# A list schedule that makes GpSimd and VectorE take turns, loads V and weights behind K, and closes with a fence

## The chip, the cores and the metric

The kernel runs on one NeuronCore of a Trainium2 chip. The metric is the device time of one execution in microseconds (us). The median of three runs before the change is 532.61 us (532.23 to 536.52). The engines are named as the profile names them: PE (TensorE, matrix products), DVE (VectorE), ACT (ScalarE), POOL (GpSimd) and SP (the queue that issues most DMA loads). PE writes to PSUM, of which this kernel uses eight banks, four tagged "a" and four tagged "t".

## The reference

Three layers follow each other on B=2 batches of S=768 rows:

```
scores = q k^T / 8 + bias;  keep = (first n_global columns) or (0 <= row - column < n_local)
a = softmax(where(keep, scores, -1e9));  x = a v                # 8 heads of 64
h = (x^T U V)^T;  u = x + h                                     # U: 768x32, V: 32x768
x = u + relu(u w_ch1) w_ch2                                     # 512 -> 2048 -> 512
k = relu(mix(x, mu_k) w_k)^2;  r = sigmoid(mix(x, mu_r) w_r);  out = r * (k w_v)
```

mix(x, mu) = mu * x + (1 - mu) * (x shifted by one row). n_global is 8 and n_local is 96, so a block of 128 rows needs a narrow band of K columns and the first few.

## The kernel before, in words

**Front.** Attention runs on eight pairs of heads (four pairs p for each of two batches b, numbered pp = 0 to 7), each in six blocks i of 128 rows. For a pair, SP loads Q (384 KB), K (768 KB) and V (768 KB). For each block PE makes the scores (`s`, line 433), DVE adds the bias and takes the extremum (`P`, `nm`, line 441), ACT takes the exponential (line 449), DVE inverts the sums after three blocks (`sm`, lines 454 and 455), POOL scales the rows (`P`, line 460, two steps a block), PE transposes (`tp`, line 467), and ACT or DVE copies the result out of PSUM (`PT`). After three blocks PE multiplies with the even rows of V (`xa`, `xb`, line 482, step `pa`), after six with the odd rows (line 493, step `pb`); then ACT and DVE copy `xa` and `xb` to `yp` (step `y`).

Beside that the front converts weights. They arrive as float64 in `stg` (512 KB a piece); one conversion is `cvt` (DVE, line 616), `c1` (ACT, line 621), `c2` and `c3` (DVE, lines 625 and 629), and a split into a high part (`hi`, ACT, line 633) and a low part (`lo`, POOL, line 636). Nine conversions belong to the front: one piece for U and V, four for `w1s`, four for `w2s`. When batch 0 is done, the front also transposes it (`xtp`, line 734), multiplies with U and V (`gps`, `hps`), adds h to `yp` (`hd`, `he`, line 788), splits the result (`sh` on ACT, `sl` on POOL, line 821), and does the first product with w_ch1 (`aps`, line 852, steps `ch`; `rs`, lines 856 and 860).

**What sets the order.** `Flow` (lines 52 to 138) is a list scheduler that runs while the program is built. `pairs` and `rest` give it 644 steps with a kind, a rank, the steps they need (`after`), the steps that must only be planned first (`behind`) and the buffers (`Tok`) they take or use. `COST` gives for each kind the engine, how long it holds that engine and after how long its result can be used. `run` takes again and again the step that can start first (lower rank first within `SLACK`), and emits its instructions; so each engine's queue in the front is in the planned order, and `tc.manual_schedule` keeps it so. A step that needs a buffer of a full pool waits for a fixed one: the oldest taken, whether it is free or not (line 97). The plan of before lets POOL and DVE steps run beside each other at will.

**Behind the front**, from line 984 on, no plan is made: the framework's own scheduler orders the instructions by their priority and may also put them between those of the front where the engine's queue has, by its reckoning, room. There batch 1 is transposed (`xtp`), and a steady stretch alternates `aps` (48 matmuls) and `bps` (line 874, 48 matmuls) over four groups of weights and three chunks of 512 rows, with the conversions of the next groups woven in (`bg`); then come `kps`, `prs`, `pvs` for the last layer.

Of the kernel before, what the change touches and what calls it, by code (L numbers as in the profile page):

```python
# [7 lines left out]
F32 = mybir.dt.float32  # L8
# [5 lines left out]
ALU = mybir.AluOpType  # L14
# [11 lines left out]
FLOWLOG = None  # L26
BIG = 1.0e9 * 256.0
# [24 lines left out]
class Flow:  # L52

    COST = {
# [4 lines left out]
        "nm": [("POOL", 0.42, 0.50)], "pt": [("ACT", 0.37, 0.52), ("DVE", 0.47, 0.60)],  # L61
        "y": [("ACT", 0.38, 0.54), ("DVE", 0.47, 0.60)], "xt": [("ACT", 0.49, 0.64), ("DVE", 0.60, 0.74)],
        "cvt": [("DVE", 0.40, 0.48)], "c1": [("ACT", 0.59, 0.73)], "c2": [("DVE", 0.61, 0.74)],
# [8 lines left out]
    SWITCH, SLACK, RATE, LAND = 0.13, 0.06, 400.0, 2.0  # L72

    def __init__(self, caps, now, queue):
        self.caps, self.now, self.queue = caps, dict(now), queue
        self.steps, self.order = [], {p: [] for p in caps}
# [5 lines left out]
    def taken(self, pool, n, done=0.0):  # L82
        for _ in range(n):
            t = Tok(pool)
            t.done = done
            self.order[pool].append(t)

    def ready(self, x):

        if any(a.end is None for a in (*x.behind, *x.after)):  # L90
            return None
        old, count = [], {}
# [8 lines left out]
        for eng, hold, lat in self.COST[x.kind]:  # L101
# [3 lines left out]
            out.append((max([go] + [t.done for t in old]), eng, hold, lat))  # L105
        return out

    def run(self, log=None):
        left, self.mode = list(self.steps), None
        while left:  # L110
            cand = {}
            for x in left:
                for go, eng, hold, lat in self.ready(x) or ():
                    cand.setdefault(eng, []).append((go, x, hold, lat, eng))
# [7 lines left out]
            go, x, hold, lat, eng = best  # L122
            go, eng, hold, lat = min(self.ready(x), key=lambda y: y[0] + y[3])
            x.start, x.eng, x.free = go, eng, go + hold
            self.now[eng] = go + hold
            if eng == "PE":
                self.mode = self.MODE.get(x.kind, 0)
            if eng == "SP":
                self.queue = max(self.queue, go + self.LAND) + lat / self.RATE
                x.end = self.queue  # L130
            else:
                x.end = go + lat
            for t in x.new:
                self.order[t.pool].append(t)
# [45 lines left out]
def body(tc, out, q, k, v, lim, UV, w1, w2, mu_kr, wk, wv, wr):  # L180
    nc = tc.nc
    with ExitStack() as ctx:
# [9 lines left out]
        y = yp.rearrange("p k (b s) -> p k b s", b=2)  # L192
# [107 lines left out]
        def attention_windows(pool, actx, cctx, bctx, bank, evict, rest, xt_p):  # L300
# [156 lines left out]
            def s_norm(pp, i, x):  # L457
                z = st[pp]
                Px = z["P"][i][:, 192 * (1 - x):192 * (2 - x)]
                nc.gpsimd.tensor_scalar(out=Px, in0=Px, scalar1=z["sm"][:, i, x:x + 1], scalar2=1.0,  # L460
                                        op0=ALU.mult, op1=ALU.mult)
# [40 lines left out]
            def pairs(fl):  # L502

                out, ls, lm, lt, lp, lx = [], None, None, None, None, None
                for pp in range(NPR):
                    R = 10.0 * pp
                    q, kk, vt = Tok("q"), Tok("k"), Tok("v")
                    nm, sm = Tok("nm"), Tok("sm")
                    lq = lk = None
                    if pp < 2:  # L510
                        for t in (q, kk):
                            fl.order[t.pool].append(t)
                    else:
                        lq = fl.add("dq", lambda pp=pp: load_q(pp), new=[q], rank=R - 12)
                        lk = fl.add("dk", lambda pp=pp: load_k(pp), after=[lq], new=[kk], rank=R - 12)
                    lv = fl.add("dk", lambda pp=pp: load_v(pp), new=[vt], rank=R - 4)
# [15 lines left out]
                    for h in range(2):  # L532
                        m = fl.add("sm", lambda pp=pp, h=h: s_sum(pp, 3 * h, 3 * h + 3),
                                   after=[e[i, x] for i in range(3 * h, 3 * h + 3) for x in range(2)], use=[sm], rank=R + 3 * h / 6)
                        for i in range(3 * h, 3 * h + 3):
                            n[i] = [fl.add("nm", lambda pp=pp, i=i, x=x: s_norm(pp, i, x), after=[m], use=[P[i], sm],
                                           rank=R + 2 + i / 6) for x in range(2)]
                    R += 8
                    for i in range(NT):
                        t = Tok("t")  # L540
                        a = fl.add("tp", lambda pp=pp, i=i: t_mm(pp, i), after=n[i] + [a if i else None], new=[t], use=[P[i]], rank=R + i / 6, behind=[lt, lx if i == 2 else None])
# [14 lines left out]
                return out  # L556
# [8 lines left out]
            with tc.manual_schedule(engines={mybir.EngineType.PE, mybir.EngineType.Activation, mybir.EngineType.DVE,  # L565
                                             mybir.EngineType.Pool, mybir.EngineType.SP}):
                fl = Flow({"a": 4, "t": 4, "P": 10, "PT": 8, "q": 2, "k": 2, "v": 2, "nm": 3, "sm": 3, "stg": 3, "cvt": 2,
                           "cvc": 4, "zt": ZT},
                          {"PE": 5.9, "ACT": 6.6, "DVE": 6.4, "POOL": 10.0, "SP": 3.1}, 7.6)
                fl.taken("P", 7, 6.4)  # L570
                fl.taken("t", 1, 5.9)
                fl.taken("nm", 1)
                fl.taken("sm", 1)
                rest(fl, pairs(fl))
                fl.run(FLOWLOG)

        def path(general):
            if general:
                attention_general()
            with ExitStack() as pctx:  # L580
# [25 lines left out]
                def conv_steps(shape, hi, lo, plain=None):  # L606
# [28 lines left out]
                    def low(z):  # L635
                        nc.gpsimd.tensor_tensor(out=lo, in0=z["c"].bitcast(F32), in1=hi.bitcast(F32), op=ALU.subtract)  # L636
# [174 lines left out]
                def u_split(c, kk, mk, part=None):  # L811
# [4 lines left out]
                    if part == "high" or part == "low":  # L816
# [3 lines left out]
                        else:  # L820
                            nc.gpsimd.tensor_tensor(out=u[:, 1, kk, a:e], in0=ys, in1=u[:, 0, kk, a:e].bitcast(F32),
                                                    op=ALU.subtract)
# [91 lines left out]
                else:  # L914
                    actx, bctx, cctx = ExitStack(), ExitStack(), ExitStack()

                    def rest(fl, ends):
# [3 lines left out]
                        def conversion(r):  # L921
# [3 lines left out]
                            ds = fl.add("ds", lambda: z.update(stage(src)), new=[toks["st"]], rank=r - 12)  # L925
                            d = {}
                            for kind, f in steps:
# [4 lines left out]
                                d[kind] = fl.add(kind, lambda f=f: f(z), after=after, new=[toks[x] for x in new],  # L932
# [3 lines left out]
                        uvd = conversion(24)  # L936
                        w1d = [conversion(r) for r in (34, 44, 54, 64)]
# [9 lines left out]
                        R = 41.0  # L947
# [21 lines left out]
                        for kk in range(4):  # L969
                            h = fl.add("sh", lambda kk=kk: u_split(0, kk, slot_a, "high"), after=[adds[kk, 0]], rank=R + 1)  # L970
                            sp.append([h, fl.add("sl", lambda kk=kk: u_split(0, kk, slot_a, "low"), after=[h], rank=R + 1)])
# [8 lines left out]
                    attention_windows(pool, actx, cctx, bctx, bank, evict, rest, xt_p)  # L980
# [137 lines left out]
```

## Time and profile before

| what | us |
|---|---|
| median of three runs | 532.61 |
| the profiled execution's own time | 532.49 |
| its span, first to last instruction | 530.7 |
| PE busy (95%) | 506.5 |
| DVE busy (58%) | 306.7 |
| ACT busy (41%) | 220.2 |
| POOL busy (35%) | 187.3 |

The span is the time from the first to the last instruction; 1.8 us lie around it. An engine's busy time counts its instructions, not its waits. A row of a timeline gives start, length, engine, line, operation, output and inputs; in brackets stand the idle time of the engine before the row and what ended it. "PEclk" is the TensorE clock that was granted, as a share of the full 2.4 GHz.

### The profile page before, as it was taken

To read this page: it belongs to the slowest core of one execution; us is meant where nothing else is said; L and a number is where in the kernel's file an instruction comes from. 1 tells how busy PE (TensorE), PEld (TensorE's weight loads), DVE (VectorE), ACT (ScalarE), POOL (GpSimd) and SP (SyncE) were. 2 spreads that over 40 slices of the span, in tenths; PEclk is the share of its full clock that TensorE was granted. 3 is DMA by queue.
4 is the path that set the end of the run, shared out by engine and by line. 5 is a ranking of instruction groups with operands and counts; after the bars stand their busy time and mean duration, and the time that the engine had idled before them with its cause. 6 is when DMAs were issued, how large, how long until landed. Compare 5 with 4: busy or idle time off the path is not lost.

```text
span 530.7 us, 8670 instructions
## 1 busy us (share of the span) xinstructions
PE 506.5 (95%) x3314; PEld 413.1 (78%) x3314; DVE 306.7 (58%) x665; ACT 220.2 (41%) x515; POOL 187.3 (35%) x247
## 2 busy tenths in 40 slices
PE   7789988799999999999999999999999999999995
PEld 4568667678888888888888888887888888888884
DVE  7689998749995563825547655798033623252110
ACT  6899985416532404104031321543931442044100
POOL 7577598004440402104031402644731442044100
PEclk9999999799999999999999999999999999999998
DMA  8887534500553040401304130041001000100001
GB/s 327 320 288 264 204 103 158 161 2 0 173 183 122 16 143 0 159 0 38 121 1 159 33 126 0 1 158 41 0 21 40 22 1 21 40 20 1 21 21 46
DMA packets 13586, 47.18 MB, mean 89 GB/s; under 512 B 1760, under 2 KB 2144, under 8 KB 13536
## 3 DMA queue, kind: packets, MB, share of 16 engines
q1 hardware_dynamic: 13248, 46.28, 25.5%
q8 instruction: 28, 0.46, 0.4%
q10 hardware_dynamic: 288, 0.26, 0.2%
q14 instruction: 22, 0.18, 0.1%
HBM read 43.39 MB, written 3.15 MB: 88 GB/s over the span
## 4 chain that ended last, share of the span: by engine, by line
PE 77%; DVE 12%; DMA 5%; ACT 1%; issue 1%; POOL 1%; SPq 0%; DVEq 0%; POOLq 0%; ACTq 0%
PE aps L852 23%; PE bps L874 21%; PE pvs L1057 12%; PE kps L1027 10%; PE prs L1046 6%; DMA KK<-in_k_dram 5%; DVE cvc L625 3%; DVE cvc L629 2%; DVE P L441 1%; PE tp L467 1%; DVE cvt L616 1%; PE s L433 1%; DVE yp L878 1%; DVE xt L686 1%; DVE mix L1014 1%
## 5 line engine op out<-in xcount | busy, mean ns | idle before, releaser
L852 PE MATMUL aps<-us,w1s 128*128 128x512 f32 x576 | 133.3, 390 | 0.0
L874 PE MATMUL bps<-rs,w2s 128*128 128x512 f32 x576 | 132.5, 389 | 0.0
L874 PEld LDWEIGHTS bps<-rs,w2s 128*128 128x128 f32 x576 | 108.1, 188 | 23.2 <-PE gps L752 0.8
L852 PEld LDWEIGHTS aps<-us,w1s 128*128 128x128 f32 x576 | 107.9, 188 | 22.2
L856 ACT ACTIVATE rs<-aps 128x512 fp32r<-128x512 f32 x48 | 28.1, 593 | 92.9 <-PE aps L852 92.9
L1027 PE MATMUL kps<-mix,wk 128*128 128x512 f32 x288 | 66.1, 389 | 0.5 <-ACT kf L1031 0.5
L1027 PEld LDWEIGHTS kps<-mix,wk 128*128 128x128 f32 x288 | 54.0, 188 | 12.1 <-ACT kf L1031 0.9
L1057 PE MATMUL pvs<-wv,kh 128*128 128x512 f32 (+1 forms) x208 | 61.9, 373 | 0.0
L625 DVE SCALAR_TENSOR_TENSOR cvc<-cvc,cvt 128x512 uint32<-128x512 uint32 (+1 forms) x53 | 51.1, 965 | 8.8 <-ACT cvc L621 7.7
L860 DVE SCALAR_TENSOR_TENSOR rs<-aps,rs 128x512 fp32r<-128x512 f32 x48 | 32.6, 684 | 39.4 <-ACT rs L856 39.4
L621 ACT ACTIVATE cvc<-stg 128x512 f32<-128x512 f32 (+1 forms) x53 | 35.1, 671 | 48.4 <-DMA stg<-in_w_dram 22.7
L878 DVE TENSOR_TENSOR yp<-bps,yp 128x512 f32<-128x512 f32 (+1 forms) x64 | 33.9, 550 | 31.2 <-PE bps L874 31.2
L460 POOL TENSOR_SCALAR P<-P,sm 128x192 f32<-128x192 f32 x96 | 45.0, 489 | 19.4 <-ACT P L449 7.7
L1009 POOL TENSOR_SCALAR mixt<-yp,mu 128x512 f32<-128x512 f32 (+1 forms) x32 | 21.5, 678 | 74.2 <-DVE mixf L1011 29.6
L636 POOL TENSOR_TENSOR w1s<-cvc,w1s 128x512 fp32r<-128x512 f32 x16 | 23.8, 1505 | 62.5 <-ACT w1s L633 62.5
L629 DVE SCALAR_TENSOR_TENSOR cvc<-stg,cvc 128x512 uint32<-128x512 uint32 x52 | 45.4, 880 | 0.8
L636 POOL TENSOR_TENSOR w2s<-cvc,w2s 128x512 fp32r<-128x512 f32 x16 | 24.0, 1526 | 60.8 <-ACT w2s L633 57.7
L449 ACT ACTIVATE P<-P,nm 128x192 f32<-128x192 f32 x96 | 42.6, 449 | 3.0 <-DVE nm L441 2.9
L1057 PEld LDWEIGHTS pvs<-wv,kh 128*128 128x128 f32 x208 | 38.1, 188 | 6.9
L1037 POOL TENSOR_TENSOR kl<-kf,kh 128x512 fp32r<-128x512 f32 x24 | 31.0, 1292 | 30.6 <-ACT kh L1036 30.6
L1057 PE MATMUL pvs<-wv,kl 128*128 128x512 f32 (+1 forms) x104 | 38.8, 373 | 0.0
L1011 DVE SCALAR_TENSOR_TENSOR mixf<-yp,mu,mixt 128x512 f32<-128x512 f32 (+1 forms) x32 | 20.3, 653 | 29.8 <-POOL mixt L1009 29.7
(113 smaller groups left out, 594.7 us busy)
## 6 DMA issues: line engine op xcount, KB each, us to landing
stg<-in_w_dram SPq DMA_DIRECT2D x32, 512.0 KB, 4.2
vin<-in_v_dram SPq DMA_DIRECT2D x8, 768.0 KB, 5.8
KK<-in_k_dram SPq DMA_DIRECT2D x7, 768.0 KB, 6.9
stg<-in_wk_dram SPq DMA_DIRECT2D x8, 512.0 KB, 4.2
stg<-in_wv_dram SPq DMA_DIRECT2D x8, 512.0 KB, 3.7
out_dram<-sg SPq DMA_DIRECT2D x11, 256.0 KB, 2.0
QS<-in_q_dram SPq DMA_DIRECT2D x7, 384.0 KB, 5.5
stg<-in_wr_dram SPq DMA_DIRECT2D x4, 512.0 KB, 4.0
```

The costliest lines, as they stand in the source:

```text
L449: nc.scalar.activation(out=Px, in_=Px, func=ACTF.Exp, scale=-1.0, bias=z["nm"][:, i, x:x + 1], accum_out=z["sm"][:, i, x:x + 1])
L460: nc.gpsimd.tensor_scalar(out=Px, in0=Px, scalar1=z["sm"][:, i, x:x + 1], scalar2=1.0, op0=ALU.mult, op1=ALU.mult)
L621: nc.scalar.activation(out=z["c"].bitcast(F32), in_=parts(z)[1].bitcast(F32), func=ACTF.Copy, scale=2.0 ** -112)
L625: nc.vector.scalar_tensor_tensor(out=z["c"], in0=z["c"], scalar=3, in1=z["t"], op0=ALU.logical_shift_left, op1=ALU.bitwise_or)
L629: nc.vector.scalar_tensor_tensor(out=z["c"] if plain is None else plain, in0=parts(z)[1], scalar=0x80000000, in1=z["c"], op0=ALU.bitwise_a ...
L636: nc.gpsimd.tensor_tensor(out=lo, in0=z["c"].bitcast(F32), in1=hi.bitcast(F32), op=ALU.subtract)
L852: nc.tensor.matmul(rs[g, c, f], lhsT=wsl(("w1", g), lw, kk, f * 128, 128), rhs=us[c][:, lx, kk, :], start=(kk == 0 and n == 0), stop=(kk = ...
L860: nc.vector.scalar_tensor_tensor(out=r[:, 1, f, :], in0=rs[g, c, f], scalar=0.0, in1=r[:, 0, f, :].bitcast(F32), op0=ALU.max, op1=ALU.subt ...
L874: nc.tensor.matmul(ps, lhsT=wsl(("w2", g), lw, f, o * 128, 128), rhs=r[:, lx, f, :], start=(n == 0), stop=(n == 11))
L878: nc.vector.tensor_tensor(out=ys, in0=ps[:, a:e], in1=ys, op=ALU.add)
L1027: nc.tensor.matmul(ps, lhsT=wsl("wk", lw, kk, f * 128, 128), rhs=xk[:, lx, kk, :], start=(n == 0), stop=(n == 11))
L1057: nc.tensor.matmul(pv, lhsT=ks[c][lx][:, f, t * 128:(t + 1) * 128], rhs=wsl("wv", lw, f, c0, c1 - c0), start=(n == 0), stop=(n == 23))
```

## The change

The planner is changed, the steps are the same 644. (1) A common time `port` is kept: a POOL step, and a DVE step of the kinds in `PORT`, starts only when the one before it of either engine has ended. Three kinds that were POOL's alone (`nm`, `lo`, `sl`) may go to DVE at a penalty. (2) Q and K of the pairs 2 to 7 are added ahead of everything else; a V load is `behind` the V before it and the K of the next pair, a weight load `behind` a K. (3) A pool gives the buffer whose last user was planned longest ago among those that are free. (4) The first product with V (`pa`) needs no longer all six transposes planned first, nor the third transpose the product; the third and fourth group of `ch` wait for the last scores. (5) A fence: whatever is traced behind the front is issued, on PE, ACT, DVE and POOL, behind the front's last instruction on that engine.

```diff
     COST = {
-        "nm": [("POOL", 0.42, 0.50)],
+        "nm": [("POOL", 0.40, 0.46), ("DVE", 0.25, 0.36, 1.2)],
-        ... "lo": [("POOL", 1.25, 1.35)], ... "sl": [("POOL", 1.15, 1.25)],
+        ... "lo": [("POOL", 1.28, 1.38), ("DVE", 0.62, 0.75, 1.5)], ... "sl": [("POOL", 1.25, 1.35), ("DVE", 0.62, 0.75, 1.5)],
...
-    SWITCH, SLACK, RATE, LAND = 0.13, 0.06, 400.0, 2.0
+    PORT = {("DVE", k) for k in ("cvt", "c2", "c3", "sm", "nm", "lo", "sl", "small")}
+    SWITCH, SLACK, RATE, LAND = 0.13, 0.06, 390.0, 2.1
...
-        for t in x.new:
-            n = len(self.order[t.pool]) + count.get(t.pool, 0) - self.caps[t.pool]
-            count[t.pool] = count.get(t.pool, 0) + 1
-            if n >= 0:
-                old.append(self.order[t.pool][n])
-        if any(u.end is None for t in old for u in t.users):
-            return None
+        for pool in {t.pool for t in x.new}:
+            free = [t for t in self.live[pool] if all(u.end is not None for u in t.users)]
+            free.sort(key=lambda t: max([u.turn for u in t.users], default=-1))
+            n = sum(t.pool == pool for t in x.new) + len(self.live[pool]) - self.caps[pool]
+            if n > len(free):
+                return None
+            old += free[:max(n, 0)]
...
+            if eng == "POOL" or (eng, x.kind) in self.PORT:
+                go = max(go, self.port)
...
+            if eng == "POOL" or (eng, x.kind) in self.PORT:
+                self.port = go + hold
...
+                loads = {}
+                for pp in range(2, NPR):
+                    loads[pp] = [Tok("q"), Tok("k")]
+                    lq = fl.add("dq", lambda pp=pp: load_q(pp), new=loads[pp][:1], rank=10 * pp - 12)
+                    loads[pp].append(fl.add("dk", lambda pp=pp: load_k(pp), after=[lq], new=loads[pp][1:2], rank=10 * pp - 12))
...
-                    lv = fl.add("dk", lambda pp=pp: load_v(pp), new=[vt], rank=R - 4)
+                    lv = fl.add("dk", lambda pp=pp: load_v(pp), new=[vt], rank=R - 4, behind=[lv, loads[pp + 1][2] if 0 < pp < NPR - 1 else None])
...
-                        a = fl.add("tp", ..., behind=[lt, lx if i == 2 else None])
+                        a = fl.add("tp", ..., behind=[lt])
...
-                    last = a
+                    last = None
...
                 fl.run(FLOWLOG)
+                ends = {x.engine: x for x in nc.cur_bb.bb.instructions}
+                return [ends[e] for e in (mybir.EngineType.PE, mybir.EngineType.Activation, mybir.EngineType.DVE,
+                                          mybir.EngineType.Pool)]
...
-                        uvd = conversion(24)
-                        w1d = [conversion(r) for r in (34, 44, 54, 64)]
+                        uvd = conversion(24, lks[0])
+                        w1d = [conversion(r, lk) for r, lk in zip((34, 44, 54, 64), lks[1:])]
...
-                                           new=[t] if kk == 0 else [], use=[t], rank=100 + f)
+                                           new=[t] if kk == 0 else [], use=[t], rank=100 + f,
+                                           behind=[last_s] if f >= FB else [])
...
-                    attention_windows(pool, actx, cctx, bctx, bank, evict, rest, xt_p)
+                    for x in attention_windows(pool, actx, cctx, bctx, bank, evict, rest, xt_p):
+                        fence.enter_context(tc.issue_after(x))
```

Three places of the new order follow; line numbers of the changed kernel are some 10 to 20 higher for the same statement. The first is DVE at the end of the front, where the front's own last steps are the `rs`, `PT`, `hps` and `yp<-xb` rows. Before:

```order
296 L860 SCALAR_TENSOR_TENSOR rs<-aps,rs 128x512
297 L616 TENSOR_SCALAR cvt<-stg 128x512
298 L625 SCALAR_TENSOR_TENSOR cvc<-cvc,cvt 128x512
299 L616 TENSOR_SCALAR cvt<-stg 128x512
300 L629 SCALAR_TENSOR_TENSOR cvc<-stg,cvc 128x512
301 L860 SCALAR_TENSOR_TENSOR rs<-aps,rs 128x512
302 L625 SCALAR_TENSOR_TENSOR cvc<-cvc,cvt 128x512
303 L616 TENSOR_SCALAR cvt<-stg 128x512
304 L629 SCALAR_TENSOR_TENSOR cvc<-stg,cvc 128x512
305 L625 SCALAR_TENSOR_TENSOR cvc<-cvc,cvt 128x512
306 L686 COPY yp<-xb 128x6x64
307 L788 TENSOR_TENSOR yp<-hps,yp 128x256 x4
```

And now:

```order
296 L705 COPY yp<-xb 128x6x64
297 L705 COPY PT<-tp 128x384
298 L634 TENSOR_SCALAR cvt<-stg 128x512
299 L705 COPY PT<-tp 128x384
300 L643 SCALAR_TENSOR_TENSOR cvc<-cvc,cvt 128x512
301 L647 SCALAR_TENSOR_TENSOR cvc<-stg,cvc 128x512
302 L705 COPY yp<-xb 128x6x64
303 L634 TENSOR_SCALAR cvt<-stg 128x512 x2
304 L643 SCALAR_TENSOR_TENSOR cvc<-cvc,cvt 128x512
```

Counted from the start, row 295 of before is the front's ninth and last `c3`; the `cvt`, `c2` and `c3` of rows 297 to 305 except the `rs` belong to the weights behind the front (`w1s` of group 1). Now rows 298, 300 and 301 are the front's ninth conversion, and the foreign ones begin at row 303, behind the last `yp<-xb`. The addition `yp<-hps` for the columns 512 to 767 is done further ahead.

The second place is ACT in the same stretch. Before:

```order
86 L621 ACTIVATE cvc<-stg 128x512
87 L856 ACTIVATE rs<-aps 128x512
88 L621 ACTIVATE cvc<-stg 128x512
89 L684 COPY yp<-xa 128x6x64
90 L621 ACTIVATE cvc<-stg 128x512
91 L684 COPY PT<-tp 128x384 x3
92 L684 COPY yp<-xa 128x6x64
```

And now:

```order
75 L876 ACTIVATE rs<-aps 128x512 x4
76 L703 COPY yp<-xa 128x6x64
77 L703 COPY PT<-tp 128x384
78 L651 CAST w2s<-cvc 128x512
79 L703 COPY PT<-tp 128x384
80 L703 COPY yp<-xa 128x6x64
81 L651 CAST w2s<-cvc 128x512
82 L639 ACTIVATE cvc<-stg 128x512
```

The three `cvc<-stg` of before in rows 86, 88 and 90 are conversions behind the front; now the first of them is row 82, behind the last `yp<-xa`.

The third place is SP from the V load of pair 0 on (`vin` is V, 768 KB a load; `stg<-in_w` 512 KB, `stg<-in_UV` 384 KB). Before:

```order
6 L329 DMA vin<-in_v_dram 128x1536 x2
7 L703 DMA stg<-in_UV_dram 128x384
8 L666 DMA stg<-in_w_dram 128x512
9 L206 DMA mu<-in_mu_dram 128x8
10 L666 DMA stg<-in_w_dram 128x512
11 L318 DMA QS<-in_q_dram 128x768
12 L324 DMA KK<-in_k_dram 128x1536
```

And now:

```order
6 L340 DMA vin<-in_v_dram 128x1536
7 L217 DMA mu<-in_mu_dram 128x8
8 L685 DMA stg<-in_w_dram 128x512 x3
9 L1115 TENSOR_LOAD flag_i
10 L1115 ISA x2
11 L329 DMA QS<-in_q_dram 128x768
12 L335 DMA KK<-in_k_dram 128x1536
13 L340 DMA vin<-in_v_dram 128x1536
```

The second V load moved behind the K of pair 2, the U and V piece further down, and a third `stg<-in_w` ahead. The load of the flag that chooses the program's path, which stood behind the K of pair 3, now stands ahead of the Q of pair 2.

## Rows read from the trace of the kernel before

**Rows 1.** Stretches: busy us (instructions) of PE, PEld, DVE, ACT, POOL; clock; DMA; GB/s.
```profile
0.00:21.20 21.20, 15.01 (x221) 9.42 (x221) 13.47 (x79) 16.47 (x62) 15.46 (x58) 1.00 0.92 350
21.20:62.30 41.10, 38.11 (x764) 29.95 (x766) 36.58 (x159) 38.51 (x141) 27.69 (x57) 1.00 0.70 254
62.30:91.20 28.90, 25.84 (x341) 20.13 (x330) 27.36 (x72) 22.95 (x66) 24.82 (x33) 1.00 0.42 132
91.20:102.30 11.10, 6.49 (x110) 5.63 (x111) 9.58 (x19) 3.35 (x7) 0.44 (x1) 0.69 0.60 184
...
102.30:530.70 428.40, 421.07 (x1898) 348.02 (x1892) 219.70 (x338) 138.91 (x241) 118.91 (x100) 1.00 0.17 55
```

**Rows 2.** PE's waits from 0 to 103 us: us in total, times, longest.
```profile
PE s L433 <- DMA KK<-in_k_dram: 5.2, 5, 2.1
PE tp L467 <- POOL P L460: 4.1, 5, 1.2
PE hps L783 <- ACT yp L684: 3.8, 1, 3.8
```

**Rows 3.** Timeline of PE at the end of the front.
```profile
95.00 0.58 PE L783 MATMUL hps<-uv 96*128 96x256 f32 x1 [3.80 <-ACT yp L684]
96.39 0.58 PE L783 MATMUL hps<-uv 96*128 96x256 f32 x1 [0.81 <-DVE yp L686]
96.81 2.79 PE L467 MATMUL tp<-ident,P 128*128 128x128 f32 x12
```

**Rows 4.** Timeline of ACT, 93 to 96 us.
```profile
93.91 0.67 ACT L621 ACTIVATE cvc<-stg 128x512 f32<-128x512 f32 x1 [2.36 <-DMA stg<-in_w_dram]
94.48 0.47 ACT L684 COPY yp<-xa 128x384 f32<-128x384 f32 x1
```

**Rows 5.** Timeline of DVE, 90 to 96 us.
```profile
90.62 1.57 DVE L625 SCALAR_TENSOR_TENSOR cvc<-cvc,cvt 128x512 uint32<-128x512 uint32 x1
...
93.66 0.67 DVE L625 SCALAR_TENSOR_TENSOR cvc<-cvc,cvt 128x512 uint32<-128x512 uint32 x1
...
95.79 0.54 DVE L686 COPY yp<-xb 128x384 f32<-128x384 f32 x1
```

**Rows 6.** Stretch, as Rows 1, around the fall of the clock.
```profile
93.50:100.40 6.90, 4.59 (x30) 3.86 (x32) 5.51 (x13) 3.00 (x6) 0.00 (x0) 0.51 0.67 183
```

**Rows 7.** Timeline of PE, rows between 14 and 67 us.
```profile
14.83 0.55 PE L467 MATMUL tp<-ident,P 128*128 128x128 f32 x3 [1.18 <-POOL P L460]
...
21.20 1.53 PE L433 MATMUL s<-KK,QS 64*64 64x192 f32 x32 [1.66 <-DMA KK<-in_k_dram]
...
30.51 1.53 PE L467 MATMUL tp<-ident,P 128*128 128x128 f32 x12
...
40.21 0.99 PE L433 MATMUL s<-KK,QS 64*64 64x192 f32 x16 [2.13 <-DMA KK<-in_k_dram]
...
66.61 1.12 PE L467 MATMUL tp<-ident,P 128*128 128x128 f32 x6 [1.11 <-POOL P L460]
```

**Rows 8.** Stretch, as Rows 1, ahead of the scores of pair 2.
```profile
18.00:21.00 3.00, 1.54 (x72) 1.33 (x68) 0.91 (x3) 3.00 (x14) 2.43 (x7) 1.00 1.03 424
```

**Rows 9.** Timeline of POOL: the flag, the low parts of w2s.
```profile
10.02 0.21 POOL L219 TENSOR_SCALAR flag_i<-flag_f 1x1 int32<-1x1 f32 x1
...
84.17 4.86 POOL L636 TENSOR_TENSOR w2s<-cvc,w2s 128x512 fp32r<-128x512 f32 x3
90.31 1.34 POOL L636 TENSOR_TENSOR w2s<-cvc,w2s 128x512 fp32r<-128x512 f32 x1 [1.28 <-ACT w2s L633]
```

**Rows 10.** POOL by line: count, min/median/max ns, first and last start.
```profile
L460 POOL TENSOR_SCALAR P<-P,sm x96: 418/425/1372, 10.5 to 82.8; 128x192 f32<-128x192 f32 x96
L636 POOL TENSOR_TENSOR w1s<-cvc,w1s x4: 1271/1274/1287, 41.7 to 75.0; 128x512 fp32r<-128x512 f32 x4
```

**Rows 11.** Stretches, as Rows 1, just behind the front.
```profile
102.30:107.00 4.70, 4.70 (x42) 3.01 (x36) 3.32 (x8) 3.74 (x9) 0.00 (x0) 1.00 0.37 115
107.00:120.00 13.00, 12.57 (x58) 10.12 (x56) 6.18 (x12) 2.52 (x6) 0.00 (x0) 1.00 0.00 1
```

More of the change, by code (lines that the diff above doesn't have):

```diff
@@ L26 @@
 FLOWLOG = None
+UR = 41.0
+FB = 2
 BIG = 1.0e9 * 256.0
@@ L85, in taken @@
             t.done = done
-            self.order[pool].append(t)
+            self.live[pool].append(t)
     def ready(self, x):
@@ L112, in run @@
             for x in left:
-                for go, eng, hold, lat in self.ready(x) or ():
-                    cand.setdefault(eng, []).append((go, x, hold, lat, eng))
+                for go, eng, _, _, later, _ in self.ready(x) or ():
+                    cand.setdefault(eng, []).append((go + later, x))
             assert cand, [(x.kind, x.rank) for x in left][:9]
@@ L132, in run @@
                 x.end = go + lat
+            for t in old:
+                self.live[t.pool].remove(t)
             for t in x.new:
-                self.order[t.pool].append(t)
+                self.live[t.pool].append(t)
+            x.turn = len(self.steps) - len(left)
             left.remove(x)
@@ L506, in pairs @@
                     R = 10.0 * pp
-                    q, kk, vt = Tok("q"), Tok("k"), Tok("v")
+                    q, kk, vt = *(loads[pp][:2] if pp in loads else (Tok("q"), Tok("k"))), Tok("v")
                     nm, sm = Tok("nm"), Tok("sm")
-                    lq = lk = None
+                    lk = loads[pp][2] if pp in loads else None
                     if pp < 2:
                         for t in (q, kk):
[L512 to L515, printed above, removed]
-                    lv = fl.add("dk", lambda pp=pp: load_v(pp), new=[vt], rank=R - 4)
+                            fl.live[t.pool].append(t)
+                    lv = fl.add("dk", lambda pp=pp: load_v(pp), new=[vt], rank=R - 4, behind=[lv, loads[pp + 1][2] if 0 < pp < NPR - 1 else None])
                     e, P, PT, X, tp, o = {}, {}, {}, [Tok("t"), Tok("t")], {}, []
@@ L540, in pairs @@
                         t = Tok("t")
-                        a = fl.add("tp", lambda pp=pp, i=i: t_mm(pp, i), after=n[i] + [a if i else None], new=[t], use=[P[i]], rank=R + i / 6, behind=[lt, lx if i == 2 else None])
+                        a = fl.add("tp", lambda pp=pp, i=i: t_mm(pp, i), after=n[i] + [a if i else None], new=[t], use=[P[i]], rank=R + i / 6, behind=[lt])
                         lt = a
@@ L555, in pairs @@
                                 for x in range(2)])
-                return out
+                return out, [loads[pp][2] for pp in range(2, NPR)], ls
             wins = masks()
@@ L579, in path @@
                 attention_general()
-            with ExitStack() as pctx:
+            with ExitStack() as pctx, ExitStack() as fence:
                 def pool(name, bufs, side=None, stack=pctx):
@@ L633, in high, with low @@
                         nc.scalar.copy(out=hi, in_=z["c"].bitcast(F32))
-                    def low(z):
-                        nc.gpsimd.tensor_tensor(out=lo, in0=z["c"].bitcast(F32), in1=hi.bitcast(F32), op=ALU.subtract)
+                    def low(z, eng="POOL"):
+                        engine = nc.vector if eng == "DVE" else nc.gpsimd
+                        engine.tensor_tensor(out=lo, in0=z["c"].bitcast(F32), in1=hi.bitcast(F32), op=ALU.subtract)
                     return [("cvt", cvt), ("c1", c1), ("c2", c2), ("c3", c3)] + ([("hi", high), ("lo", low)] if plain is None else [])
@@ L809, in path, with u_split @@
                 us = {}
-                def u_split(c, kk, mk, part=None):
+                def u_split(c, kk, mk, part=None, eng=None):
                     if c not in us:
@@ L915, in path, with rest, conversion @@
                     actx, bctx, cctx = ExitStack(), ExitStack(), ExitStack()
-                    def rest(fl, ends):
+                    def rest(fl, ends, lks, last_s):
                         fl.add("dm", constants, rank=30)
                         fl.add("small", complement, after=[fl.steps[-1]], rank=30)
-                        def conversion(r):
+                        def conversion(r, behind=None):
                             src, steps = bgq.pop(0)
@@ L924, in conversion @@
                             toks = {"st": Tok("stg"), "t": Tok("cvt"), "c": Tok("cvc")}
-                            ds = fl.add("ds", lambda: z.update(stage(src)), new=[toks["st"]], rank=r - 12)
+                            ds = fl.add("ds", lambda: z.update(stage(src)), new=[toks["st"]], rank=r - 12, behind=[behind])
                             d = {}
```

39 lines of the change are left out of this document (22 added, 17 removed), and 2 rows, old and new, of the table COST.

## The prediction

> **What bounds the kernel now.** I read the stretches first [rows 1], to see where PE, the busiest engine, still stands still. From 102.30 to the end it is busy 421.07 of 428.40 us; little is to be had there. The front, 102.30 us long, has PE busy 85.45 us, so 16.85 us idle: 6.19 before 21.20, 2.99 up to 62.30, 3.06 up to 91.20, and 4.61 of only 11.10 us after that. This last stretch also has a granted clock of 0.69. All that a new order of the front can give lies in these idle times and in that clock.
>
> Next the waits of PE there [rows 2]. The scores wait five times for K (5.2 us), the transposes five times for the scaled `P` of POOL (4.1), one `hps` waits 3.80 us for ACT's `yp<-xa`, and the next 0.81 us for DVE's `yp<-xb` [rows 3]. The last two make the whole 4.61.
>
> Then I asked what ACT and DVE did while PE waited. ACT had a `cvc<-stg` directly ahead of `yp<-xa`, and that had stood 2.36 us for a weight's DMA [rows 4]. It is a conversion from behind the front, put by the framework's scheduler into a queue in which a copy was due. DVE likewise had steps of these conversions, 0.67 us each, directly ahead of `yp<-xb` [rows 5]. PE pays twice: from 93.50 to 100.40 the granted clock is 0.51, the 1.2 GHz level, with PE busy 4.59 us [rows 6], and it fell behind the idle time that began at 91.20.
>
> **The change part by part. A, the fence.** It keeps all these conversions behind the front's last instruction on their engine; in the new order the copies of `xa` and `xb` stand ahead of every foreign row on ACT and DVE. Without the wait for the weight's DMA the copies can follow PE. Of the idle 4.61 us I leave 0.6, about one copy (0.54 [rows 5]) that PE has to wait for: 4.0 gained. The clock: twelve transposes took 2.79 us at the low level [rows 3] and 1.53 at the high one [rows 7], so at least 1.26 is lost, and at most half of 4.59, which is 2.3; I take the middle, 1.8. Together **A = −5.8 us**. Its ends are 0 (the copies come late for another reason and the clock falls as before) and −6.4 (4.1 + 2.3).
>
> **B, turns, loads and transposes.** Here PE's waits from 14 to 91 us count. K: 1.4 of the 5.2 us are the first three waits at the start, whose loads are not moved; left are 1.66 at 21.20 and 2.13 at 40.21 [rows 7]. POOL: 1.11 at 66.61, one as long 13 us later, and three in all of 4.1 − 2.2 = 1.9 between 14 and 17 us, the longest 1.18 [rows 7]. That is 3.8 + 4.1 = 7.9 us.
>
> The first third of it (1.66 + 1.9) I book at nothing. In the new order of SP, 640 KB fewer stand between the K of pair 1 and that of pair 2 (one V and the U and V piece move behind it, one weight ahead: 768 + 384 − 512). At the 424 GB/s of that time [rows 8] K lands 1.5 us earlier. The new flag load ahead of it waits only for POOL's flag, written at 10.02 [rows 9]; the queue is busy up to 21, so it is covered. But the work that covers the wait is gone as well: pair 0's first product with V now stands ahead of its last transposes, where it fills POOL's waits, and its second behind the scores of pair 2. PE will have nothing from about 17 to 19.7 us, when K lands; what was won ahead of the gap is lost in it.
>
> The other 4.4 us (2.13 + 1.11 + 1.11) can go: the wait at 40.21 is for K of pair 5, whose first scores now stand on PE behind eighteen transposes and a part of a product with V that were behind them, and whose load has a V and the 384 KB of U and V ahead of it where it had a V and a 512 KB weight; and POOL's `P` take a median of 0.425 us, but one took 1.372 [rows 10], which is what taking turns should end. The lock that turns are about shows in two rows: a DVE step on two SBUF inputs took 1.57 us at 90.62, while POOL's 1.34 us stood beside it [rows 9], and 0.67 with POOL idle [rows 5]. Turns remove no work, though: who waited inside an instruction now waits ahead of it. I take two thirds of 4.4: **B = −3.0 us**, with ends 0 and −5.6 (all 4.4, and a third of the first third).
>
> The choice of DVE for `nm`, `lo` and `sl` is void: in the new order all 96 + 8 + 4 of these steps still stand on POOL. Of the copies `PT`, 6 move from ACT to DVE; no wait of PE for a `PT` is among the large ones [rows 2], so I give it nothing.
>
> **D, the conversions behind the fence.** Four conversions of the next weights, which before ran in part ahead of 102.30, must now fit behind it. They have twelve DVE steps of at most 0.67 us, 8.0 us. DVE is free 1.38 + 6.82 = 8.2 us up to 120 [rows 11]. It just fits, so something will be late: the additions that free PSUM banks for PE, or the low parts. I take one step and a little, **D = +0.8 us**; ends 0 and +2.7 (four times 0.67).
>
> Sum against the profiled execution: 532.49 − 5.8 − 3.0 + 0.8 = **524.5 us**. That execution stands 0.12 below the median, which I neglect.
>
> **Rivals.** R1, the clock falls in the new gap. PE stands 2 to 3 us before the scores of pair 2; at the end of the front it stood 3.80 and 0.81 us with 0.58 between, and the clock fell during that. For it: the gap is longer than the 1.66 us at that place before, after which the clock was 1.00. Against it: the 2.13 at 40.21 left it at 1.00 too [rows 1]. If it falls for 6.9 us as it did [rows 6], with PE busy 38.11/41.10 of the time, it costs up to 6.9 × 0.93 / 2 = 3.2, at least the 1.8 of part A; 2.5 gives 527.0 us. [...]
>
> R2, only the fence counts: B = 0, as the wait on POOL moves from the inside of an instruction to the place ahead of it, and the transposes now ahead of pair 5's scores wait for `P` as long as these did for K. 532.5 − 5.8 + 0.8 = 527.5 us. For it: DVE is busy 36.58 and ACT 38.51 of 41.10 us [rows 1], so that chain has little slack. Against it: half of the 4.4 us is a wait for a load, which turns do not touch, and DVE's busy share was lower, 13.47 of 21.20, where three of the waits for `P` were. The Trainium skill, "SBUF — State Buffer", section "Who interferes with whom", says that the shared pair of ports is an exclusive lock, and issue order decides which of the two is held up; the 1.57 us at 90.62 agrees, and by this rule turns choose the loser and save nothing, which is this rival.
>
> R3, the change does not do what it says: the copies of `xa` and `xb` were late through PE's own order or the loads, not through the foreign steps, so A is near −1, and B about −1: 530 to 531 us. Against it: the wait of 2.36 us stands in the very row ahead of the copy [rows 4].
>
> R4, slower. In the new order POOL has a block of four `us` low parts and two of `w2s` between two `P` steps of the last pairs: 4 × 1.27 [rows 10] + 2 × 1.62 (4.86 for three [rows 9]) = 8.3 us. It decides if the scores and `aps` that PE has there last less than that: PE then idles up to 8 us, say 5, the clock falls (+1.8), and what the fence gave is lost with D at its end: 532.5 − 5.8 + 5 + 1.8 + 2.7 + 1.5 for the K gap = 537.7 us. Against it: PE had 25.84 us of work in 28.90 there [rows 1], and three low parts in one piece, 4.86 us, at 84.17 were covered.
>
> **How the numbers follow.** Chances: the forecast 0.52, R1 0.21, R2 0.15, R3 0.07, R4 0.05. The likeliest case alone lies from 521.3 (A −6.4, B −5.0, D +0.2) to 526.5 (−5.0, −2.0, +1.0). With R1 and most of R2 the range is 521.3 to 529.0; R3, R4 and thin ends of the others, under 0.2, are outside. A measurement of this kernel can tell about 1%, 5.3 us, from no change; faster by that means under 527.3: 0.95 of the forecast, 0.65 of R1, 0.45 of R2, together 0.70. Slower is R4, 0.05; the rest, 0.25, is within 1%.
>
> **What would show it.** A: no `cvc` ahead of the last `yp<-xa` and `yp<-xb`, under 1 us of PE idle at the last `hps`, clock 1.00 there. B: no wait of over 1 us for K of pair 5 or for `P` behind 60 us; a gap of 2 to 3 us ahead of the scores of pair 2, and whether the clock holds behind it. D: PE idle within the first 20 us behind the front, put down to DVE or POOL by more than before. I am wrong if PE's idle time in the front stays above 12 us, or if the 428.40 us behind it grow by over 2.

## The result and the profile after

The changed kernel takes **527.80 us** (median; all its runs lie within 0.07 us) where the kernel before took 533.55 in the runs beside it: a ratio of 0.9885 (95% interval 0.984 to 0.993), 5.8 us less. The prediction said 524.5, range 521.3 to 529.0. The number lies in the range, but above 526.5, where the likeliest case alone ended; it is 3.3 us from the forecast, 0.8 from the rival R1 (527.0) and 0.3 from R2 (527.5). It is 1.15% below the runs beside it, just over the 1% that the chances were about, but above 527.3, where the prediction set that 1%. From the profiled execution of before (532.49), where the sum began, to that of the change (527.80) it is 4.7 us.

The stretches up to the first `bps` and behind it, of the kernel before (columns as in [rows 1]):

```profile
0.00:107.00 107.00, 90.16 (x1458) 68.13 (x1458) 90.30 (x335) 85.02 (x283) 68.41 (x147) 0.97 0.64 227
107.00:530.70 423.70, 416.38 (x1859) 345.01 (x1856) 216.38 (x331) 135.16 (x232) 118.91 (x100) 1.00 0.17 54
```

and of the changed kernel, with the two stretches that parts A and B spoke of:

```profile
0.00:101.50 101.50, 91.59 (x1458) 67.66 (x1458) 81.23 (x328) 82.26 (x278) 63.66 (x147) 0.98 0.60 219
101.50:526.00 424.50, 416.45 (x1857) 344.94 (x1856) 222.06 (x341) 136.13 (x234) 118.40 (x100) 1.00 0.18 59
19.62:25.00 5.38, 5.38 (x121) 4.44 (x121) 3.57 (x22) 2.44 (x10) 2.13 (x6) 0.68 0.51 203
88.23:97.04 8.81, 8.15 (x198) 7.14 (x197) 8.43 (x15) 4.66 (x11) 2.99 (x6) 1.00 0.24 68
```

The first `bps` begins 5.50 us earlier, and 0.80 is given back behind it. PE is idle 9.91 us ahead of it instead of 16.84 (107.00 − 90.16), but it is busy 1.43 us longer for the same 1458 matmuls. Of this 0.87 us stand in the first 14 us, where PE is busy 11.83 us instead of 10.96 and is hardly further for it (119 matmuls instead of 115). The slow stretch of [rows 6] is gone: 88.23 to 97.04 has clock 1.00. A new one stands at 19.62, clock 0.68. PE's waits of the changed kernel in this time, which answer to [rows 2]:

```profile
PE s L444 <- DMA KK<-in_k_dram: 2.2, 1, 2.2
PE xtp L753 <- ACT xt L703: 1.8, 1, 1.8
...
PE tp L479 <- POOL P L472: 1.1, 4, 0.4
PE tp L479 <- ACT yp L703: 0.7, 1, 0.7
PE s L444 <- DVE nm L452: 0.6, 2, 0.5
PE aps L872 <- DVE nm L452: 0.6, 1, 0.6
PE gps L771 <- DVE xt L712: 0.5, 1, 0.5
```

K went from five waits to one (three of the five were the short ones in the first 14 us), `P` from 4.1 us to 1.1, and no `hps` waits for a copy there. New are 1.8 us at `xtp` and five smaller waits of 2.4 us in all. The one wait for K is the gap that the prediction saw coming (PE's timeline, answering to [rows 7]):

```profile
16.89 0.55 PE L479 MATMUL tp<-ident,P 128*128 128x128 f32 x3 [0.26 <-POOL P L472]
19.62 2.25 PE L444 MATMUL s<-KK,QS 64*64 64x192 f32 x32 [2.19 <-DMA KK<-in_k_dram]
```

The 32 scores took 2.25 us instead of 1.53: the clock had fallen. And the wait at `xtp` is the old fault in a new place. ACT and SP of the changed kernel:

```profile
47.57 0.47 ACT L703 COPY yp<-xa 128x384 f32<-128x384 f32 x1
49.88 0.70 ACT L639 ACTIVATE cvc<-stg 128x512 f32<-128x512 f32 x1 [1.84 <-DMA stg<-in_w_dram]
...
51.80 2.00 ACT L703 COPY xt<-xtp 128x512 f32<-128x512 f32 x4
```

```profile
4.42 1.62 SPq L685 DMA_DIRECT2D stg<-in_w_dram  x3
...
35.18 0.33 SPq L722 DMA_DIRECT2D stg<-in_UV_dram  x1
...
42.71 4.76 SPq L685 DMA_DIRECT2D stg<-in_w_dram  x2
```

ACT stands for a weight's DMA with the copies `xt`, for which PE waits, queued behind it; now it is a weight of the front itself. The three loads at 4.42 are pieces of `w2s`, which have no K to wait for. They fill all three `stg` buffers, so that the U and V piece, loaded at 4.54 before, now loads at 35.18, and the first piece of `w1s` at 42.71.

### The profile page after: what moved, and what is told of

It reads as the page before. It is cut to its first block, busy times and chain, and to the rows that moved or that the text cites. A ratio compares the mean times of both kernels' runs of the same rounds, so it can differ in the third digit from the quotient of the medians.

```text
span 526.0 us, 8658 instructions
## 1 busy us (share of the span) xinstructions
PE 508.0 (97%) x3314; PEld 412.6 (78%) x3314; DVE 303.3 (58%) x668; ACT 218.4 (42%) x512; POOL 182.1 (35%) x247
## 4 chain that ended last, share of the span: by engine, by line
PE 78%; DVE 7%; ACT 6%; DMA 5%; issue 1%; POOL 1%; SPq 0%; POOLq 0%; ACTq 0%
PE aps L872 24%; PE bps L894 19%; PE pvs L1079 12%; PE kps L1049 10%; PE prs L1068 6%; ACT P L460 3%; DMA stg<-in_wv_dram 2%; DMA stg<-in_w_dram 2%; DMA KK<-in_k_dram 2%; DVE cvc L643 1%; DVE cvc L647 1%; PE s L444 1%; ACT PT L703 1%; PE warm L360 1%; ACT cvc L639 1%
## 5 line engine op out<-in xcount | busy, mean ns | idle before, releaser
L472 POOL TENSOR_SCALAR P<-P,sm 128x192 f32<-128x192 f32 x96 | 41.1, 448 | 25.0 <-DVE sm L466 12.0
```

Of the source, the lines that this page charges most:

```text
L472: engine.tensor_scalar(out=Px, in0=Px, scalar1=z["sm"][:, i, x:x + 1], scalar2=1.0, op0=ALU.mult, op1=ALU.mult)
```

## The experiments

Each is timed against the kernel before on the same chip. Medians in us; the ratio with its 95% interval; last the time of the profiled execution, from which the rows of a kernel are:

| kernel | time | before | ratio | profiled |
|---|---|---|---|---|
| the change | 527.80 | 533.55 | 0.9885 (0.984 to 0.993) | 527.80 |
| fence_only | 528.02 | 533.51 | 0.9883 (0.9851 to 0.9915) | 528.57 |
| no_fence | 527.42 | 533.51 | 0.988 (0.985 to 0.991) | 527.48 |
| gap_warm | 526.23 | 533.51 | 0.9859 (0.9829 to 0.9889) | 524.36 |
| c1_held | 529.93 | 533.51 | 0.9918 (0.9888 to 0.9948) | 530.91 |
| no_turns | 532.61 | 533.07 | 0.9983 (0.996 to 1.0006) | 533.24 |
| no_behind | 525.65 | 533.07 | 0.9845 (0.9801 to 0.989) | 526.08 |
| w2_late | 525.51 | 533.07 | 0.9856 (0.9809 to 0.9902) | 523.99 |
| pv_order | 528.07 | 533.07 | 0.9904 (0.9875 to 0.9933) | 526.96 |
| turns_only | 530.07 | 533.88 | 0.9922 (0.9897 to 0.9946) | 530.16 |
| fence_turns | 527.75 | 533.88 | 0.9893 (0.9868 to 0.9918) | 527.21 |
| nb_warm | 527.30 | 533.88 | 0.9871 (0.9844 to 0.9898) | 527.32 |
| w2_nofence | 526.78 | 533.88 | 0.9858 (0.9828 to 0.9888) | 527.51 |

Of two variants, differences under about 3 us are not resolved by these intervals; where I use one, a row of the trace has to carry it.

**fence_only**, the old order with the fence:

```diff
+                ends = {x.engine: x for x in nc.cur_bb.bb.instructions}
+                return [ends[e] for e in (mybir.EngineType.PE, mybir.EngineType.Activation, mybir.EngineType.DVE,
+                                          mybir.EngineType.Pool)]
...
+                    for x in attention_windows(pool, actx, cctx, bctx, bank, evict, rest, xt_p):
+                        fence.enter_context(tc.issue_after(x))
```

> The kernel before with the fence alone; its order of the front is the old one. If the conversions from behind the front made the copies of xa and xb late (theory: the fence carries the gain), the two waits of 3.80 and 0.81 us at the last hps shrink to under 1 us, the clock there stays at 1.00, the first bps starts about 101.5 instead of 107.0, and the time is 526.7 to 528.5 us. If it was the order of PE or the loads (rival: the new order carries it), the waits stay and the time is 531 to 533 us.

5.5 us less, as the theory had it. PE's timeline at the end of its front, which answers to [rows 3]:

```profile
92.51 1.02 PE L786 MATMUL hps<-uv 96*128 96x256 f32 x3
93.78 0.38 PE L786 MATMUL hps<-uv 96*128 96x256 f32 x1 [0.25 <-DVE yp L689]
94.20 1.70 PE L467 MATMUL tp<-ident,P 128*128 128x128 f32 x12
```

Of 4.61 us of waiting 0.25 is left, and the twelve transposes take 1.70 instead of 2.79. The foreign steps were the cause. But the first `bps` begins only at 103.44, not at 101.5: in this execution the clock fell to 0.50 behind a wait of 1.25 us for `P` at 15.14, and to 0.57 from 40 to 44 us behind 2.31 us of waiting for K.

**no_fence**, the change without its fence: the last two lines above taken out again, the call left.

> The changed kernel without the fence. Two cvc<-stg of foreign conversions then stand on ACT ahead of the last two yp<-xa, and foreign c2 and c3 on DVE ahead of yp<-xb. Theory (the fence carries the gain): they wait for their weight's DMA as before, PE idles 2 to 4 us more at the end of the front, 530 to 532.5 us. Rival (the new order carries it and the fence only moves conversions): the copies are in time all the same, within 0.7 us of the changed kernel's 527.8.

The rival holds: 527.42. ACT, and PE just behind:

```profile
95.34 0.67 ACT L639 ACTIVATE cvc<-stg 128x512 f32<-128x512 f32 x1 [2.79 <-DMA stg<-in_w_dram]
95.91 0.47 ACT L703 COPY yp<-xa 128x384 f32<-128x384 f32 x1
```

```profile
94.60 0.88 PE L753 MATMUL xtp<-ident,yp 128*128 128x128 f32 x6
96.43 2.80 PE L753 MATMUL xtp<-ident,yp 128*128 128x128 f32 x18 [0.96 <-ACT yp L703]
```

The foreign step stands 2.79 us ahead of `yp<-xa` as before. Yet PE waits 0.96 us, not 3.80: in the new order the `hps` are done before, and PE has products and six `xtp` left. The fence and the new order cure one and the same wait.

**no_turns**: `PORT = set()`, and both tests of it off.

> The changed kernel planned without the common time of POOL and DVE (PORT empty, POOL free). Theory (turns choose who waits and save nothing): within 0.8 us of the changed kernel's 527.8, and PE's waits for POOL's P as small, under 1.5 us in all. Rival (turns carry what B gave): PE's waits for P come back to 3 us or more, 529.5 to 531 us.

532.61: my theory is wrong and the rival right, the time even above its 531, and its interval does not touch that of the change. A line of PE's waits, two rows of DVE and two of POOL in it:

```profile
PE tp L479 <- POOL P L472: 6.4, 11, 1.5
```

```profile
81.74 1.34 DVE L643 SCALAR_TENSOR_TENSOR cvc<-cvc,cvt 128x512 uint32<-128x512 uint32 x1
83.11 1.66 DVE L647 SCALAR_TENSOR_TENSOR cvc<-stg,cvc 128x512 uint32<-128x512 uint32 x1
```

```profile
81.24 1.29 POOL L655 TENSOR_TENSOR w1s<-cvc,w1s 128x512 fp32r<-128x512 f32 x1
82.49 1.74 POOL L655 TENSOR_TENSOR w2s<-cvc,w2s 128x512 fp32r<-128x512 f32 x1
```

A DVE step that takes 0.67 alone takes 1.34 and 1.66 beside POOL's, and POOL's low part 1.74 instead of 1.29. The lock costs busy time on both sides, and a plan that does not know of it puts the later steps too early. Besides the order, two more things differ in this run: a `P` and a `w2s` step moved from POOL to DVE, as the choice between the engines stayed open, and the clock fell a second time, to 0.50 at 46 us behind 1.38 us of waiting for `P`. POOL's steps by line, first of the changed kernel and then of no_turns (busy us, mean ns, idle before):

```profile
L472 POOL TENSOR_SCALAR P<-P,sm 128x192 f32<-128x192 f32 x96 | 41.1, 448 | 25.0 <-DVE sm L466 12.0 <-ACT P L460 6.2 <-DVE sm L465 4.9
```

```profile
L472 POOL TENSOR_SCALAR P<-P,sm 128x192 f32<-128x192 f32 x95 | 45.1, 494 | 28.7 <-DVE sm L466 10.2 <-ACT P L460 6.8 <-ACT yp L703 3.5
```

**turns_only** and **fence_turns**, to see if turns and fence add: the old kernel with `PORT = {("DVE", k) for k in ("cvt", "c2", "c3", "sm", "small")}` and its two tests, without and with the fence.

> The kernel before with the common time of POOL and DVE alone (PORT without the three kinds that may change engine), no fence, old loads, old pool rule and old bonds. Theory (turns are the part that carries the new order's gain, as the changed kernel without them is back at 532.6): 527 to 529.5 us, with PE's waits for P at 1.5 us or less. Rival (turns only repair what the other parts of the new order spoil): 531.5 to 534 us.

> The kernel before with the turns and the fence, nothing else. Theory (fence and turns act on different waits and add, and the parts left out, the loads behind K above all, cost about 2 us): 523.5 to 526 us. Rival (both remove the same lateness at the end of the front): 527 to 528.5 us, as either alone.

Turns alone give 3.8 us (530.07, between the two expectations), fence alone 5.5, both together 6.1 (527.75, the rival). So they do not add: 9.3 against 6.1, a difference hardly larger than what the intervals resolve. The change, which has the loads, the pool rule and the bonds besides, takes no less than the two alone (527.80). `P` misses its expectation: PE waits 2.5 us for it in turns_only, 2.1 of them between 14 and 17 us; these go with the bonds of the first product with V (pv_order below has them again), while the two waits of 1.11 behind 60 us are gone with turns. Without the fence the foreign steps still cost, at `xtp` 1.96 us for `yp<-xb` and 0.40 for `yp<-xa`, and the clock is 0.60 from 100 to 104 us. With it, other waits stand where the gain should be, and the clock fell to 0.51 at 17 us (PE's waits of fence_turns):

```profile
PE tp L472 <- POOL P L465: 3.0, 5, 1.3
PE s L438 <- DVE uv L730: 1.5, 1, 1.5
PE aps L860 <- DVE nm L446: 1.5, 1, 1.5
PE hps L791 <- ACT uv L781: 1.2, 1, 1.2
...
PE xtp L742 <- ACT xt L699: 1.1, 1, 1.1
```

All but the first are for DVE and ACT, which in the changed kernel's front are busy 80% and 81% of the time.

**gap_warm**, the gap filled so that only the clock changes:

```diff
                 sps = z["s", i // 2]
+                if pp == 2 and i == 0:
+                    for _ in range(9):
+                        nc.tensor.matmul(sps[0].rearrange("p i n -> p (i n)"), lhsT=wz[:, 0:128], rhs=wz, start=True, stop=True)
```

> The changed kernel with nine matmuls on zeros into the scores' own bank ahead of pair 2's first scores, where PE stands 2.19 us for K; nothing else is moved. Theory (the gap lowers the clock, which costs about 1.7 us of PE time from 19.62 to 26): the 32 scores there take 1.5 instead of 2.25 us at clock 1.00, and 526.2 to 526.8 us. Rival (the chain over DVE, ACT and POOL sets the pace behind the gap, so a faster PE only waits): the clock is back but the time stays at 527.4 to 528.

526.23, the theory; its four runs (524.36 to 526.76) lie below the four of the change, but the intervals overlap. The profiled execution, the fastest, took 524.36. Its rows answer to the two of the gap above:

```profile
16.74 2.10 PE L442 MATMUL s<-wz 128*128 128x512 bf16 x9
19.12 1.53 PE L447 MATMUL s<-KK,QS 64*64 64x192 f32 x32 [0.28 <-DMA KK<-in_k_dram]
```

With PE busy through the gap the clock stays at 1.00 and the scores take 1.53. So it was the gap that lowered it, and 0.72 of 2.25 us is its price on these 32 alone. The first `bps` begins at 98.73, 2.8 us earlier than in the change, as the wait at `xtp` shrank too (0.7). The stretch up to it:

```profile
0.00:98.73 98.73, 90.88 (x1468) 66.90 (x1468) 80.83 (x328) 82.49 (x278) 63.22 (x147) 1.00 0.63 226
```

**w2_late**, w2s behind a K as well:

```diff
-                            conversion(r)
+                            conversion(r, lks[2])
```

> The changed kernel with the four pieces of w2s, too, behind a K (that of pair 4). In the changed kernel three of them load at 4.4 us, which puts 1536 KB ahead of pair 2's K and fills all three staging buffers until their conversions, so the U and V piece loads at 35.2 us and w1s from 42.7 on. Theory (these three early loads make both the 2.19 us gap with its fall of the clock and ACT's 1.84 us wait with PE's 1.81 us at xtp): K's wait under 0.7 us, clock 1.00 throughout, xtp's wait under 0.5 us, 523.5 to 525.5 us. Rival (the staging is only moved: w2s is then late at the end of the front, and the pairs' chain sets the pace before): the waits turn up later, 527 to 529 us.

525.51. PE's timeline, and the stretch up to the first `bps`, in the profiled execution (523.99, the fastest of four; two of the others took 526.58 and 526.37 with a mean clock of 0.993 and 0.992):

```profile
16.58 1.53 PE L444 MATMUL s<-KK,QS 64*64 64x192 f32 x32
...
23.52 1.02 PE L444 MATMUL s<-KK,QS 64*64 64x192 f32 x16 [1.86 <-DMA KK<-in_k_dram]
```

```profile
0.00:98.10 98.10, 88.00 (x1458) 65.19 (x1458) 81.57 (x329) 81.09 (x275) 66.29 (x147) 1.00 0.64 226
```

Pair 2's scores start 3 us earlier with no wait, the clock is 1.00 in the whole front, and PE waits for nothing at the `xtp` of batch 0. So both faults of the change come from the three early loads: without them both are gone. New are a wait of 1.86 for a later K and 1.1 at the `xtp` of batch 1; the first `bps` begins at 98.10.

**no_behind** (both lists empty), **nb_warm** (that and the matmuls of gap_warm) and **w2_nofence** (w2_late without the fence):

> The changed kernel with V and the weights free again to load ahead of a K (both behind lists out). Theory (the K gap at 19.6 and the late weight at 49.9 eat what this part gives): the U and V piece and w1s load earlier, ACT does not wait for a weight around 48 us and PE waits under 0.5 us at xtp, but K of a later pair is late by 1 to 2 us: 526.5 to 528.5 us. Rival (K ahead of V is worth its 4.4 us of K and P waits): 529.5 to 531.5 us.

> The changed kernel without both behind lists and with the nine matmuls on zeros ahead of pair 2's scores, where PE stood 2.43 us for K and the clock fell to 0.50. Theory (free loads and the clock add): 1.5 us less than the free loads alone, 523.5 to 524.8 us. Rival (behind the gap the chain over DVE, ACT and POOL sets the pace): 525.2 to 526 us.

> The changed kernel with w2s behind the K of pair 4 (525.5 us) and without the fence; on ACT one foreign cvc<-stg then stands ahead of the last yp<-xa. Theory (in the new order the fence is nearly worth nothing, as no hps waits behind that copy any more): within 0.6 us of 525.5. Rival (with the front faster the foreign weight's DMA is late by more): 526.5 to 529 us.

no_behind takes 525.65, less than either expectation, so no gain of loading V and weights behind K shows in this order; its scores of pair 2 waited 2.43 us for K, and the clock fell just the same. nb_warm was to take 1.5 us off that and took 1.65 more (527.30, in neither expectation): the gap at 19 us is gone, but another came, and the clock fell behind that one. PE, and the stretch behind it:

```profile
37.69 0.82 PE L447 MATMUL s<-KK,QS 64*64 64x192 f32 x13
40.70 1.94 PE L447 MATMUL s<-KK,QS 64*64 64x192 f32 x19 [2.18 <-issue]
```

```profile
40.70:47.00 6.30, 6.30 (x73) 5.24 (x76) 3.20 (x17) 3.52 (x13) 1.81 (x3) 0.73 0.24 90
```

w2_nofence has 526.78, in the interval of its rival (526.5 to 529), but its runs go from 524.9 to 529.0; it doesn't tell theory and rival apart.

**pv_order** (`behind=[lt, lx if i == 2 else None]`, `last = a`) and **c1_held** (one conversion issued behind the `xt` copies):

> The changed kernel with the old bonds of the transposes and the first product with V (product behind all six transposes, third transpose behind the product before). Theory (the gap ahead of pair 2's scores came from moving pair 0's product ahead): the product fills it, PE waits under 0.8 us for that K, the clock holds, 526 to 527 us. Rival (the old bonds bring back the waits for P between 14 and 17 us, and the sum is as before): 527.5 to 529 us.

> The changed kernel with one conversion's steps (cvt, c1, c2, c3, hi of the first piece of w1s) issued behind the six xt copies of batch 0 instead of ahead of them; in the changed kernel ACT stood 1.84 us at 48 us for that piece's DMA with the xt copies behind it, and PE 1.81 us at xtp. Theory (that wait is on the path): PE's wait at xtp falls under 0.5 us and the time to 526.0 to 526.8 us. Rival (the pairs' chain is late by as much anyway): the wait turns up at the next transposes, 527.4 to 528.2 us.

pv_order, 528.07: the rival. The gap is filled and the clock held, but PE waits 3.0 us for `P` again. c1_held, 529.93, is above both expectations, so its theory falls in the form I gave it: the wait at `xtp` is gone, but PE stands 1.82 us for `P` at 54.77. The late thing is the load, and whichever step of it comes first stands there: DVE, which had a `cvt` of the next piece ahead, now stood 3.16 us and with it the sums that POOL waits for.

```profile
53.33 0.43 DVE L642 TENSOR_SCALAR cvt<-stg 128x512 uint32<-128x512 uint32 x1 [3.16 <-DMA stg<-in_w_dram]
```

## Why the prediction was right, and where not

The sum came to −7.0 us of PE's idle time (4.0 of A, 3.0 of B), −1.8 of its busy time (the clock of A) and +0.8 behind (D). The stretches up to the first `bps`, and the rest of the spans (522.6 us for gap_warm, 522.1 for w2_late), show what came of each, against before; of gap_warm the 2.10 us of the nine matmuls on zeros are counted as idle:

| us | PE idle | PE busy | behind |
|---|---|---|---|
| forecast | −7.0 | −1.8 | +0.8 |
| the change | −6.9 | +1.4 | +0.8 |
| gap_warm | −6.9 | −1.4 | +0.2 |
| w2_late | −6.7 | −2.2 | +0.3 |

So what is missing in the change is mostly PE's busy time: the clock that was won back at the end of the front was lost again in the new gap. Where the clock held, the terms of the front come near the forecast, and so do these two executions (524.36 and 523.99); they are the fastest of their kernels, whose medians are 526.23 and 525.51. The idle time of the change flatters it: 0.87 us of it turned into busy time in the first 14 us and gained next to nothing; without them it is −6.1 and +0.6.

- **A, the fence.** The mechanism is right: alone it removes 4.36 of the 4.61 us and the low clock there. Its size of 5.8 (5.5 measured alone) stands, but I booked it to the fence only. The new order holds the same gain without it, so in the change the fence by itself is worth nothing that can be measured.
- **B.** The waits of B went as forecast or better (K of pair 5 from 2.13 to none, `P` from 4.1 to 1.1), but what came instead (1.8 at `xtp`, 0.6 twice, 0.7, 0.5) took most of it back. What I called the first third, and booked at nothing, is 3.56 of 7.9 us, nearly half. A and B were also added as if their parts were independent; turns and fence in the old order do not look so. "Turns remove no work" misled: a step held up by the lock is busy time. Over the whole program DVE and POOL are busy 3.4 and 5.3 us less than before (81.23 + 222.06 and 63.66 + 118.40, from the stretches above). In no_turns they are busy 305.11 and 185.00 us, so 1.8 and 2.9 more than in the change, although two of POOL's steps stand on DVE there; and the gain is gone. By the Trainium skill, "SBUF — State Buffer", section "Who interferes with whom", issue order decides who of the two is held up. The 1.34, 1.74 and 1.66 us of no_turns agree, each step beginning while one of the other engine still ran; that nothing is saved, which I drew from it for R2, does not follow.
- **R1.** The gap came where and as long as forecast (17.4 to 19.62, K landing at 19.6 for an expected 19.7), and the clock fell. This is the step on which the forecast was off: I gave it 0.21 and it happened. From 19.62 to 25.00 PE was busy 5.38 us at 0.68, at most 1.7 us lost, and gap_warm is 1.6 us faster; I had taken 2.5.
- **R2.** Its number is the nearest (527.5), but by luck: `P` did not take K's place as the wait ahead of pair 5's scores, and without turns 4.8 us are lost.
- **D.** +0.8 was forecast and +0.80 stands there, but it is not shown that the conversions make it: gap_warm, with the same order, has 423.87 us behind the first `bps`, fence_only 423.26, before 423.70. What the trace does show of them stands ahead of that `bps`. Behind the fence nobody plans turns; a foreign `c2` runs beside a low part on POOL, takes 1.53 us, and the copy `xt` behind it is the one that `gps` waits for. DVE, POOL and PE of the changed kernel:

```profile
97.14 1.53 DVE L643 SCALAR_TENSOR_TENSOR cvc<-cvc,cvt 128x512 uint32<-128x512 uint32 x1
98.59 0.68 DVE L712 COPY xt<-xtp 128x512 f32<-128x512 f32 x1
```

```profile
96.59 1.53 POOL L655 TENSOR_TENSOR w2s<-cvc,w2s 128x512 fp32r<-128x512 f32 x1 [2.25 <-ACT w2s L651]
```

```profile
99.33 2.25 PE L771 MATMUL gps<-xt,uvf 128*32 128x512 f32 x12 [0.54 <-DVE xt L712]
```

- **R3** and **R4** did not come: the block of six low parts on POOL was covered, with 0.57 us of waiting near it.
- What stays open: how much each part is worth by itself. The variants between 525.5 and 528.1 us overlap in their intervals, and each removed wait brought up another. V's and the weights' bonds were not tried apart, the pool rule and the Q and K loads moved ahead not alone. Two versions, no_behind and w2_late, have lower medians than the change by some 2 us, but do not stand clear of it.

## What to carry to other kernels

Gains from removing waits need not add, as fence and turns did not here: ask of each part what is left of the wait once the other is done, and try each alone. A load that is put behind others must come with a rule for who may hold its buffers meanwhile; here the pieces needed last took all three. When a plan pulls work ahead to fill a small wait, look at the gap that the work used to cover, and give the clock behind that gap a term of its own in the sum.

## What was not expected of the hardware

In the middle of one group of scores PE stopped for 2.18 us with nothing in the profile to wait for (rows of nb_warm above), while the DMA engines were 95% busy with loads. Such a stop, of 0.5 to 2.24 us and not always at the same instruction, stands in six more of the profiled executions between 37 and 46 us. The queue named "instruction" had a packet between 38.0 and 38.5 us, where the stop begins, but in the kernel before it has one at 44 us and PE does not stop; that the loads keep instructions waiting is argued, not shown.

In this stretch, at 19.62, and in w2_nofence the clock fell behind a single stop of 2.2 us, while 1.66 and 2.13 us had left it at 1.00 before the change [rows 7]. The length of one stop does not tell it, though: it also fell behind 1.66 us at 19.34 in no_turns and behind 1.02 us at 19.47 in c1_held, each with three stops of some 0.3 us for `P` shortly before, and it held behind 1.43 us at 41.49 in no_behind.
